# A new order, planned buffers and TensorE transposes of x in a fused attention and gated FFN kernel

## The chip, the cores and the metric

The kernel runs on one NeuronCore of a Trainium2 chip. The metric is device time in microseconds (us). Three runs of the kernel before took 385.79, 387.66 and 388.32 us; the median is 387.66 us. A separate profiled execution gives the trace that is read below. The core has TensorE (PE: matrix products into eight PSUM banks), VectorE (DVE), ScalarE (ACT), GpSimd (POOL) and SyncE (SP), which here only issues DMAs. Each engine works through its own instruction list strictly in the order that the program gives; semaphores make it wait for others.

## What is computed

A linear attention with an exponential feature map, then a gated FFN (ReLU gate times value). Shapes: q, k, v are 8 batches x 8 heads x 576 positions x 64; the feature width is 128 (256 with the mirrored half); the FFN goes 512 to 1536 to 512 on 4608 rows.

```python
def phi(x):
    proj = np.einsum('bhsd,df->bhsf', x, w_phi)
    proj = proj - np.max(np.abs(proj), axis=-1, keepdims=True)
    return np.concatenate([np.exp(proj), np.exp(-proj)], axis=-1)
q_p, k_p = (phi(q), phi(k))
kv = np.einsum('bhsf,bhsd->bhfd', k_p, v)
z = np.sum(k_p, axis=2)
num = np.einsum('bhsf,bhfd->bhsd', q_p, kv)
den = np.einsum('bhsf,bhf->bhs', q_p, z)[..., None] + 1e-06
x = (num / den).transpose(0, 2, 1, 3).reshape(B * S, H * D)
out = (np.maximum(x @ w_gate, 0.0) * (x @ w_val)) @ w_out
```

## The kernel before

The whole program is one long word list, `ORDER`. Each word names a step, its indices and the PSUM banks that it uses; `kr.1.0:0672` is step `do_kr` for batch 1, head group 0, in banks 0, 6, 7 and 2. The last lines of the kernel walk the list and call the steps, and that order is the order of every engine's instruction list and of every DMA queue. Nothing else schedules. Buffers are rings: the n-th use of a tile name takes tile n modulo the ring's size.

A batch has 512 main positions (four tiles of 128) and 64 left over; the leftovers of two batches make one mixed tile, called batch 8. So the FFN has nine groups of 512 rows: batches 0 to 7 and group 8. Heads come in groups of 2, 3 and 3.

The steps of one batch, with the engine that does each:

- Loads. POOL issues those of k (`lk`), q (`lq`), their leftovers (`lm`, `ln`), v of batch 0 (`lv.0`), and the weights in thirds: `wl.0.i` is third i of `wv`, `wl.1.i` of `wg` (512 of 1536 columns each), `wo.i` third i of `wo`. SP issues v of the other batches (`lv`), its leftovers (`lw`), and `gt`, a small transfer that the next k load on POOL waits for. v of batch 1 lands in a free part of the tile that later holds x transposed (`xTs`).
- k features. DVE transposes k in blocks (`kt`, `ku`), PE multiplies by w_phi (`kr`), ACT takes exponentials with both signs (`ke`), DVE takes the maximum of absolute values (`kx`), ACT turns it into scales (`kk`), POOL scales v with them (`vs`, `vr`, and `vo` for the column of ones). For batch 0 PE transposes k itself (`k0`), DVE copies it from PSUM (`k1`), PE multiplies (`k2`), and DVE scales one head group (`kp` on ACT, `vd` and `vp` on DVE).
- kv (`kv`, PE), copied from PSUM by ACT (`kc`) or DVE (`kd`).
- q features. `qt` (DVE transpose), `qc` or `qs` (PE), `qe` (ACT), `qx` (DVE maximum), then `qy` (PE), `qz`, `qu` (DVE) and `qw` (ACT), which give the factor between the two halves. `mt` to `mw` are the same for the mixed tile.
- Numerator and denominator, per position tile i and head group: `nu` (PE), `nt` and `nv` (DVE combine the two halves), `nr` (DVE reciprocal), `nx` (normalise on POOL) or `ny` (the same on DVE) writes tile `xu`.
- x transposed to `xTs`: `xt` is a DMA transpose issued by SP. For batch 0, tiles 0 and 1, it is PE (`xp`, four 128x128 transposes into a PSUM bank) and a copy by DVE (`xc`).
- FFN. `fv` and `fg` are the products with a column block f (128 wide) of `wv` and `wg`, four matmuls of 512 columns each; f 8 to 11 lie in the last third of the weights. `va` copies the value product from PSUM (ACT), `ga` multiplies it with the rectified gate (DVE) into a slot of `h2` (15 slots, taken in turn). For batch 0, blocks 0 to 7 are done per position tile (`pv`, `pg`, `pa`, `pb`: 16 matmuls of 128 columns each), so that they can start before all of x is there; blocks 8 to 11 go as `fv` and `fg` and need all four tiles of x. `fo.g.t.part` is a third of the output product of tile t, `oc` copies it from PSUM (ACT), `od` writes it out (SP). A tile of group 8 is written in two DMAs of 64 rows.
- `zz.n` issues n matmuls on a tile of zeros, with no use made of the result.

The order around the change at the start, PE's list alone: `xp.0.0`, `pg.0.0`, `xp.0.1`, ..., `pv.1.2`, `pg.1.2`, `fv.0.9`, `fv.0.8`, `pv.0.3`, `qc.1.0`, ... The tiles 2 and 3 of x of batch 0 are turned by `xt.0.2` and `xt.0.3`; on SP's list three loads of batch 1's v stand between those two. At the end, group 7 comes before group 8: the last words are `fo.8.2.2`, `oc.8.2`, `od.8.2`.

Of the kernel before, what the change touches and what calls it, by code (L numbers as in the profile page):

```python
# [9 lines left out]
BF16 = mybir.dt.bfloat16  # L10
# [18 lines left out]
qy.0.0:5 qz.0.0:5 qe.0.0.1.1:6 kv.0.2:3 qx.0.0.3:2 kv.0.1:5 qe.0.1.3.0:7 qu.0.0 qe.0.0.1.0:6
qe.0.1.1.1:0 qx.0.1.2:1 kc.0.2:3 qw.0.0 kc.0.1:5 qx.0.1.3:7 wl.0.1 vs.0.0.1 qy.0.1:6 qz.0.1:6  # L30
kt.1.1 nu.0.0.2:0 vs.0.0.0 nt.0.0.2:0 qe.0.1.2.1:1 vo.0 kv.0.0:3 qe.0.1.2.0:1 kc.0.0:3
qe.0.0.3.0:2 qu.0.1 nv.0.0.2:0 qy.0.2:6 qz.0.2:6 qw.0.1 nu.0.0.1:5 nt.0.0.1:5 qe.0.1.3.1:7
qe.0.0.2.1:4 nu.0.1.1:1 nu.0.0.0:0 qu.0.2 qw.0.2 nv.0.0.1:5 qy.0.3:3 qz.0.3:3 nu.0.1.0:6 zz.2:2
kr.1.1:2537 nt.0.0.0:0 lm.1.0 nt.0.1.0:6 qe.0.0.2.0:4 nv.0.0.0:0 nt.0.1.1:1 ke.1.1.2.0:3 lq.1.2
wl.1.1 nu.0.1.2:0 nr.0.0 nu.0.2.2:4 nv.0.1.1:1 ny.0.0 nt.0.1.2:0 ke.1.1.1.0:5 nv.0.1.0:6
ke.1.1.3.0:7 ke.1.1.0.0:2 ke.1.1.1.1:5 lw.1.0 nv.0.1.2:0 zz.2:1 xp.0.0:1 wl.0.2 xc.0.0:1
nt.0.2.2:4 nr.0.1 nx.0.1 ke.1.1.2.1:3 nu.0.2.0:6 nu.0.2.1:0 qu.0.3 qw.0.3 nt.0.2.0:6 ke.1.1.3.1:7
nv.0.2.2:4 nv.0.2.0:6 ke.1.1.0.1:2 nt.0.2.1:0 pg.0.0:1 kx.1.1.1:5 nv.0.2.1:0 kx.1.1.2:3 pv.0.0:4
xp.0.1:6 nr.0.2 nx.0.2 xc.0.1:6 xt.0.2 pv.1.0:5 nu.0.3.0:0 pa.0.0:4 pb.0.0:1 pa.1.0:5 ln.0.1
pv.0.1:3 pa.0.1:3 lv.1.0 qt.1.1 kx.1.1.3:7 pg.0.1:4 nt.0.3.0:0 kx.1.1.0:2 kk.1.1.0 nv.0.3.0:0  # L40
pb.0.1:4 nu.0.3.1:6 qc.1.1:1537 qe.1.1.0.0:1 nu.0.3.2:2 qe.1.1.0.1:1 nt.0.3.1:6 qe.1.1.1.0:5
nt.0.3.2:2 qe.1.1.3.0:7 nv.0.3.1:6 pv.1.1:0 lv.1.3 nv.0.3.2:2 pg.1.1:4 pa.1.1:0 lv.1.1 nr.0.3
qx.1.1.0:1 qe.1.1.2.0:3 ln.0.0 qe.1.1.1.1:5 qx.1.1.3:7 qe.1.1.3.1:7 pg.1.0:6 pv.0.2:2 nx.0.3 ku.1
pa.0.2:2 xt.0.3 qe.1.1.2.1:3 pg.0.2:1 pb.1.0:6 kt.1.0 kr.1.0:0672 ke.1.0.1.0:6 wo.2 qx.1.1.1:5
wl.1.2 ke.1.0.3.1:2 pb.1.1:4 qx.1.1.2:3 ke.1.0.0.0:0 ke.1.0.2.1:7 ms.1 ke.1.0.2.0:7 kx.1.0.1:6
ke.1.0.1.1:6 pv.1.2:5 lm.2.0 lm.2.1 pb.0.2:1 pa.1.2:5 vs.1.1.0 wo.0 ke.1.0.0.1:0 pg.1.2:4
kx.1.0.3:2 ke.1.0.3.0:2 qt.1.0 fv.0.9:3 kk.1.1.1 kx.1.0.0:0 fv.0.8:1 pv.0.3:6 va.0.9:3 pb.1.2:4
qc.1.0:5203 vs.1.1.1 va.0.8:1 pa.0.3:6 kt.1.2 qx.1.0.1:2 kx.1.0.2:7 qe.1.0.3.0:3 qx.1.0.3:3 lk.2.3
wo.1 pv.1.3:4 qe.1.0.0.0:5 qx.1.0.0:5 qe.1.0.1.0:2 kk.1.0.0 vr.1.1.0 vs.1.0.0 vr.1.0.0
qe.1.0.1.1:2 kk.1.0.1 vo.1.0 vs.1.0.1 qe.1.0.3.1:3 pg.0.3:1 pb.0.3:1 vr.1.1.1 qe.1.0.0.1:5  # L50
pg.1.3:6 vr.1.0.1 qx.1.0.2:0 pa.1.3:4 mt.0 lv.2.3 pb.1.3:6 qe.1.0.2.0:0 fv.0.10:7 kr.1.2:2315
kx.1.2.1:3 fg.0.10:4 ke.1.2.3.1:5 kx.1.2.0:2 fv.0.11:6 qe.1.0.2.1:0 qy.1.0:0 va.0.10:7 kx.1.2.2:1
# [36 lines left out]
va.1.7:2 ga.1.7:0 vr.3.0.1 nx.2.1 fg.1.9:6 ga.1.9:6 nr.2.0 kx.3.1.1:3 ke.3.1.2.0:4 nu.2.3.2:2
ke.3.1.3.1:7 ke.3.1.0.1:1 vr.3.1.1 nx.2.0 ln.2.0 kx.3.1.3:7 ln.2.1 nu.2.3.0:4 fv.1.11:5 kt.4.0  # L90
# [146 lines left out]
def kernel(  # L237
# [11 lines left out]
    nc = tc.nc  # L249
# [730 lines left out]
```

## Time and profile before

| | before |
|---|---|
| median of three runs | 387.66 us |
| profiled execution, span from first to last instruction | 384.0 us |
| instructions | 9108 |
| PE busy (weight loads apart) | 365.5 us, 95%, 3551 matmuls |
| DVE busy | 275.2 us, 72%, 651 |
| ACT busy | 237.0 us, 62%, 566 |
| POOL busy | 160.1 us, 42%, 179 |
| moved by DMA | 38.29 MB |
| mean granted TensorE clock | 0.974 |

The three runs differ by 0.7%, and the profiled execution's span is 3.7 us below their median. Busy times are sums over the whole span and hide that its parts differ, so the table of busy time by stretch is of more use. In it and in the time line, each row begins with microseconds from the first instruction; in the time line the second number is the length, the bracket at the end of a row tells how long the engine stood idle before it and whose work ended that. A merged row (x8) holds that many instructions. A matmul's row is longer than the time it keeps the array, since its end overlaps the next; the distance from start to start tells the rate.

### The profile page before, as it was taken

The numbers are of one execution on the slowest core, as the hardware profiler recorded it, in microseconds if no ns is written. First come the engines' busy times: TensorE is split into PE (matmuls) and PEld (weight loads), VectorE is DVE, ScalarE is ACT, GpSimd is POOL, SyncE is SP. The second block draws the span as 40 slices with busy tenths as digits, with TensorE's granted clock in tenths as the row PEclk, the third lists the DMA queues.
The fourth block names the chain that finished last, engine by engine and source line by source line (L and its number), as shares of the span: only waits on it lengthen the run. The fifth ranks groups of instructions, "written<-read, shape, count | busy, mean of one in ns | idle before, by whom it ended". The sixth has DMA issues, their size and how long they took to land.

```text
span 384.0 us, 9108 instructions
## 1 busy us (share of the span) xinstructions
PE 365.5 (95%) x3551; PEld 193.7 (50%) x3551; DVE 275.2 (72%) x651; ACT 237.0 (62%) x566; POOL 160.1 (42%) x179
## 2 busy tenths in 40 slices
PE   7699679999999999999999999999999999999994
PEld 4268646545544554455545544464445544444442
DVE  4979929999997898788957797798667822521320
ACT  2987849788867915985787647964977213321321
POOL 8593729587366423672393025811462120100000
PEclk9869979999999999999999999999999999999998
DMA  8999999995965765677335742552410031000114
GB/s 131 231 167 183 181 179 154 131 127 81 215 54 124 114 106 81 122 116 109 77 88 93 134 83 65 111 102 56 112 55 2 3 82 56 27 15 0 55 63 103
DMA packets 91456, 38.29 MB, mean 100 GB/s; under 512 B 65302, under 2 KB 86550, under 8 KB 91414
## 3 DMA queue, kind: packets, MB, share of 16 engines
q0 software_dynamic: 33904, 15.23, 30.6%
q1 hardware_dynamic: 57510, 22.49, 27.4%
q8 instruction: 28, 0.46, 0.5%
q14 instruction: 14, 0.11, 0.1%
HBM read 37.95 MB, written 9.44 MB: 123 GB/s over the span
## 4 chain that ended last, share of the span: by engine, by line
PE 85%; DVE 6%; DMA 4%; SPq 1%; issue 1%; POOL 1%; ACT 0%; DVEq 0%; POOLq 0%
PE bank L865 45%; PE bank L920 25%; PE bank L618 6%; PE bank L717 3%; DMA xTs<-xu 2%; PE bank L654 2%; PE bank L476 2%; DMA qn<-in_q_dram 2%; DVE mk L531 1%; DVE t L738 1%; DVE u L748 1%; PE bank L891 1%; SPq L424 1%; DVE maxq L677 1%; PE bank L852 1%
## 5 line engine op out<-in xcount | busy, mean ns | idle before, releaser
L880 ACT CAST val<-bank 128x512 bf16<-128x512 f32 x100 | 58.0, 599 | 77.3 <-PE bank L865 56.4
L883 DVE SCALAR_TENSOR_TENSOR h<-bank,val 128x512 bf16<-128x512 f32 x100 | 66.7, 678 | 50.3 <-PE bank L865 37.0
L920 PE MATMUL bank<-wo,h 128*128 128x512 bf16 x432 | 99.0, 379 | 0.0
L523 ACT ACTIVATE kp<-bank 128x384 bf16<-128x384 f32 x192 | 81.9, 517 | 20.1 <-PE bank L476 8.3
L865 PE MATMUL bank<-xTs,wv 128*128 128x512 bf16 x352 | 88.2, 384 | 5.9 <-DMA xTs<-xu 5.7
L760 POOL TENSOR_TENSOR xu<-u,r 128x512 bf16<-128x512 f32 x35 | 36.4, 1043 | 124.4 <-DVE r L756 81.7
L865 PE MATMUL bank<-xTs,wg 128*128 128x512 bf16 x352 | 87.9, 379 | 0.0
L669 ACT ACTIVATE qp<-bank 128x512 bf16<-128x512 f32 x128 | 70.7, 627 | 4.4 <-PE bank L654 3.7
L920 PEld LDWEIGHTS <-h 128*128 128x128 bf16 x432 | 40.8, 98 | 47.7 <-issue 0.9
L865 PEld LDWEIGHTS <-wv 128*128 128x128 bf16 x400 | 37.1, 98 | 47.9 <-issue 9.7
L578 POOL TENSOR_TENSOR vs<-vn,ek 128x780 bf16<-128x780 f32 (+3 forms) x40 | 53.0, 1341 | 18.7 <-ACT ek L540 12.2
L865 PEld LDWEIGHTS <-wg 128*128 128x128 bf16 x400 | 36.6, 98 | 42.0 <-issue 3.3
L677 DVE TRANSPOSE_TENSOR_REDUCE maxq<-bank 128x16 f32<-128x512 f32 x64 | 42.4, 692 | 16.8 <-ACT val L906 7.3
L531 DVE TENSOR_REDUCE mk<-bank 128x3 f32<-128x384 f32 x96 | 49.3, 542 | 7.0 <-ACT kp L523 4.6
L929 ACT COPY ob<-bank 128x512 f32<-128x512 f32 x36 | 21.4, 598 | 29.9 <-PE bank L920 26.6
L748 DVE TENSOR_TENSOR u<-bank,t 128x195 f32<-128x195 f32 (+1 forms) x108 | 34.3, 332 | 2.7
L738 DVE TENSOR_TENSOR t<-bank,cq 128x195 f32<-128x195 f32 (+1 forms) x96 | 30.1, 327 | 3.2 <-PE bank L717 2.1
L717 PEld LDWEIGHTS <-qp 128*128 128x128 bf16 x512 | 23.8, 99 | 11.6 <-issue 0.6
L717 PE MATMUL bank<-kv,qp 128*128 128x65 bf16 x512 | 26.4, 195 | 0.2
L597 POOL TENSOR_TENSOR vr<-vm,ek 64x260 bf16<-64x260 f32 x32 | 19.7, 618 | 16.7 <-issue 9.8
L618 PEld LDWEIGHTS <-kp 128*128 128x128 bf16 x640 | 24.1, 102 | 3.3 <-DVE h L883 0.2
L618 PE MATMUL bank<-vs,kp 128*128 128x65 bf16 x512 | 24.3, 199 | 0.0
(81 smaller groups left out, 317.9 us busy)
## 6 DMA issues: line engine op xcount, KB each, us to landing
out_dram<-ob SPq DMA_DIRECT2D x32, 256.0 KB, 2.2
vn<-in_v_dram SPq DMA_DIRECT2D x24, 256.0 KB, 4.6
kn<-in_k_dram POOLq DMA_DIRECT2D x7, 512.0 KB, 8.4
qn<-in_q_dram POOLq DMA_DIRECT2D x7, 512.0 KB, 6.2
wg<-in_moe_w_gate_dram POOLq DMA_DIRECT2D x3, 512.0 KB, 8.4
wv<-in_moe_w_val_dram POOLq DMA_DIRECT2D x3, 512.0 KB, 8.6
wo<-in_moe_w_out_dram POOLq DMA_DIRECT2D x3, 512.0 KB, 13.3
vm<-in_v_dram SPq DMA_DIRECT2D x16, 64.0 KB, 4.1
```

The source lines that it names most:

```text
L523: nc.scalar.activation(kp_of(3 * b + j)[:, i, s].rearrange("p n f -> p (n f)"), bank[bk[0]][:, 0 : 3 * F], AF.Exp, scale=(1.0, -1.0)[s],)
L531: nc.vector.tensor_reduce(mk_of(3 * b + j)[:, :, i], bank[bk[0]][:, 0 : 3 * F].rearrange("p (n f) -> p n f", f=F), axis=AX.X, op=ALU.max, ...
L578: nc.gpsimd.tensor_tensor(vs_of(3 * b + j)[:, s, 0:n].rearrange("p n i e -> p (n i) e")[:, :, 0:e], src[:, lo:hi].rearrange("p h i e -> p ...
L618: nc.tensor.matmul(out_ps[:, h - lo, s, :], lhsT=lhsT, rhs=rhs, start=(at == 0), stop=(at == 2 * n * (C + 1) - 1),)
L669: nc.scalar.activation(qp_of(4 * b + i)[:, s, 4 * hq : 4 * hq + 4].rearrange("p h m -> p (h m)"), bank[bk[0]], AF.Exp, scale=(1.0, -1.0)[s],)
L677: nc.vector.tensor_reduce(maxq[:, :, i, 4 * hq : 4 * hq + 4].rearrange("p t h -> p h t"), bank[bk[0]].rearrange("p (h t u) -> p h t u", h= ...
L717: nc.tensor.matmul(bank[bk[0]][:, E * n : E * (n + 1)], lhsT=qp_of(4 * b + i)[:, s, h, :], rhs=kv_of(b)[:, h, s, :],)
L748: nc.vector.tensor_tensor(u_of(serial(b, i))[:, lo:hi], parts(bk, n)[:, :, 0], t_of(3 * serial(b, i) + g)[:, 0:n], op=ALU.add,)
L865: nc.tensor.matmul(bank[bk[0]], lhsT=w[:, dc, P * f : P * f + P], rhs=xT(g)[:, dc, :], start=(dc == 0), stop=(dc == NDC - 1),)
L880: nc.scalar.copy(val_of(NFC * g + f), bank[bk[0]])
L883: nc.vector.scalar_tensor_tensor(h2_of(g, f), bank[bk[0]], 0.0, val_of(NFC * g + f), op0=ALU.max, op1=ALU.mult)
L920: nc.tensor.matmul(bank[bk[0]], lhsT=h2_of(g, f)[:, P * t : P * t + P], rhs=wo_sb[:, f, :], start=(f == 0), stop=(f == NFC - 1),)
```

## The change

All 2040 words are put in a new order and get other banks; 2044 words come out. What differs in the steps themselves:

- Words carry buffers: `ke.0.1.1.0:1@kp0` tells which tile of a ring this use takes. The rings keep their sizes, the choice of a tile is written out. The slots of `h2` are chosen the same way (`@hs3`), apart from batch 0's twelve.
- x of batch 0: `xp.0.2`, `xp.0.3` replace `xt.0.2`, `xt.0.3`, and all four tiles are copied from PSUM by ACT (`xa`, new) instead of DVE (`xc`). `nx.0.0` replaces `ny.0.0`.
- Work moved between engines: 25 of the 100 `va` go to DVE (`vb`, new), 13 of the 36 `oc` (`oe`, now used); 12 of 18 `kd` on DVE become `kc` on ACT; six `nx` become `ny` (DVE).
- The fill `zz` has 69 matmuls instead of 42: 37 instead of 22 at the very start, 10 and 5 around the last k group of batch 0 instead of 4 and 0.
- Group 8's products are put among those of groups 6 and 7, and `fo.7.2` is the last output tile. It is copied in two halves of 256 columns, one by ACT (`o1`), one by DVE (`o2`), and written by two DMAs, one issued by SP (`d1`), one by ACT (`d2`).
- The loads move: on POOL `wl.0.2` from before `nx.0.1` to behind `nx.0.2`, `lm.1.0` and `vo.1.1`; `wl.1.2`, `wo.0` follow `nx.0.3`; `wo.1`, `wo.2` come behind `lk.2.3`. On SP `lv.1.0`, `lv.1.3` come right behind `lv.1.2`.

PE's list at the start after the change: `xp.0.0`, `kr.1.1`, ..., `pg.0.0`, `pv.1.0`, `xp.0.1`, ..., `xp.0.2`, ..., `xp.0.3`, `pv.1.2`, `kr.1.0`, `pg.1.2`, `pv.0.3`, `fv.0.9`, `fv.0.10`, ...

```diff
+    fresh = {}
+
     def ring(name, n, shape, dtype):
         tiles = [sb.tile(shape, dtype, name=f"{name}_{i}", tag=f"{name}_{i}") for i in range(n)]
-        return lambda i: tiles[i % n]
+        at = {}
+
+        def of(i):
+            if n == 1:
+                return tiles[0]
+            if i not in at:
+                at[i] = fresh.pop(name)
+            return tiles[at[i]]
+
+        return of
...
+    def do_xa(bk, b, i):
+        nc.scalar.copy(
+            xT_cols(b, i),
+            bank[bk[0]].bitcast(BF16)[:, 0 : NDC * P].rearrange("p (a b) -> p a b", b=P),
+        )
...
     def h2_of(g, f):
-        return h2[:, (NFC * g + f) % NH2]
+        i = NFC * g + f
+        if i not in h2_at:
+            h2_at[i] = fresh.pop("hs")
+        return h2[:, h2_at[i]]
...
+    def do_vb(bk, g, f):
+        nc.vector.tensor_copy(val_of(NFC * g + f), bank[bk[0]])
...
+    def do_o1(bk, g, t):
+        nc.scalar.copy(ob_of(4 * g + t)[:, 0:HD], bank[bk[0]][:, 0:HD])
+
+    def do_o2(bk, g, t):
+        nc.vector.tensor_copy(ob_of(4 * g + t)[:, HD:DM], bank[bk[0]][:, HD:DM])
+
+    def do_d1(bk, g, t):
+        r0 = S * g + P * t
+        nc.sync.dma_start(out=out[r0 : r0 + P, 0:HD], in_=ob_of(4 * g + t)[:, 0:HD])
+
+    def do_d2(bk, g, t):
+        r0 = S * g + P * t
+        nc.scalar.dma_start(out=out[r0 : r0 + P, HD:DM], in_=ob_of(4 * g + t)[:, HD:DM])
...
     for word in ORDER.split():
+        word, _, slots = word.partition("@")
         name, _, banks = word.partition(":")
         name, *args = name.split(".")
+        fresh.clear()
+        for slot in filter(None, slots.split(",")):
+            fresh[slot.rstrip("0123456789")] = int(slot[len(slot.rstrip("0123456789")) :])
```

More of the change, by code (lines that the diff above doesn't have):

```diff
@@ L227 @@
[L227 to L232 removed]
+ms.0 wp ms.6 lk.0.1 wc lq.0.1 wq ms.4@vr0 ms.3@vr1 id ms.2 wd zz.37:0 k0.1:0 k1.1:0@kT0 zz.5:1
@@ new lines @@
+qs.0.1.0:5 qt.0.0@qT1 kx.0.2.3:7 vs.0.1.1@vs0 ke.0.2.3.1:7 ke.0.0.0.0:0 ke.0.0.3.0:6 kx.0.0.3:6@mk0
+ke.0.0.1.0:3 kp.0.2.1:7 kp.0.2.0:7 kx.0.0.1:3 kx.0.0.0:0 lk.1.3 ke.0.0.0.1:0 wl.0.1 ke.0.0.1.1:3
+kx.0.0.2:2 kk.0.0.1@ek1 qs.0.0.2:1 qx.0.0.2:1 vs.0.1.0 qs.0.0.1:0 vp.2:7@vs1 kk.0.0.0
+qe.0.1.3.1:4@qp1 vd.0.2.1:7 qx.0.0.1:0 ke.0.2.3.0:7 qs.0.0.0:3 qe.0.0.0.1:3@qp2 qx.0.1.0:5
+qe.0.1.0.0:5 ke.0.0.3.1:6 wl.0.0 ke.0.0.2.1:2 qx.0.0.0:3 qe.0.1.0.1:5 vd.0.2.0:7 qs.0.0.3:6
+qe.0.0.0.0:3 qe.0.0.2.1:1@qp3 qe.0.0.1.1:0 lv.1.2 qy.0.0:2 qe.0.0.3.0:6 qx.0.0.3:6 qs.0.1.2:5
@@ new lines @@
+kx.1.1.1:3 pa.0.0:0@val1 kk.1.1.1@ek1 kk.1.1.0 xa.0.2:7 qt.1.1@qT0 ms.1 pv.0.1:1 pb.0.0:2
+pa.0.1:1@val2 pb.0.1:5 nu.0.3.1:0 nt.0.3.1:0@t0 qc.1.1:7346 qe.1.1.3.1:6@qp3 nu.0.3.2:1
+nt.0.3.2:1@t1 qe.1.1.2.1:4@qp1 pv.0.2:2 pa.0.2:2@val2 qe.1.1.0.0:7@qp0 nv.0.3.2:1 qe.1.1.0.1:7
+pg.1.0:5 kt.1.0@kT0 qe.1.1.3.0:6 nv.0.3.1:0 vo.1.1@vs2 nr.0.3@r0 qe.1.1.1.0:3@qp2 qx.1.1.3:6
+pv.1.1:2 wl.0.2 lv.1.1 nx.0.3@xu0 pg.1.1:0 pa.1.1:2@val1 xp.0.3:6 qx.1.1.0:7 lw.1.0 xa.0.3:6
+qe.1.1.1.1:3 ln.0.1 pb.1.0:5 ku.1 pv.1.2:7 pa.1.2:7@val0 lm.2.0 kr.1.0:6251 ke.1.0.1.1:2@kp0
@@ new lines @@
+xt.8.1 ln.2.0 qx.4.1.0:1 qx.4.1.1:2 vb.3.0:0@val1 fv.3.1:7 vb.3.1:7@val0 qe.4.1.3.1:5 vr.4.1.0
+vr.4.0.1 kv.4.0:1 vs.4.2.1@vs0 vs.4.1.1 fv.3.4:0 xt.8.0 od.2.1 fv.3.10:7 ga.3.0:3@hs5 fv.3.5:3
+kk.4.2.0 qx.4.1.3:5 va.3.4:0@val1 qx.4.1.2:4 qy.4.0:4 qz.4.0:4@my1 kv.4.1:0 ga.3.1:6@hs8
+kd.4.1:0@kv0 qu.4.0@mz0 ln.2.1 qe.4.1.1.0:2 vs.4.2.0 kv.4.2:4 kc.4.0:1 nu.4.0.0:0 va.3.5:3@val3
+kd.4.2:4 qw.4.0@cq0 nt.4.0.0:0@t2 qe.4.1.1.1:2 fg.3.4:6 nu.4.1.1:4 nu.4.1.2:2 nv.4.0.0:0@u0
+ga.3.4:6@hs10 fv.3.11:0 nt.4.1.2:2@t2 nv.4.1.2:2@u1 nt.4.1.1:4@t1 va.3.10:7@val0 nu.4.0.1:6
@@ new lines @@
+ke.5.1.1.0:5 fg.3.8:2 ga.3.10:3@hs7 fo.3.0.0:4 ke.5.1.1.1:5 nx.4.2@xu3 kx.5.1.0:0 kk.5.1.0@ek2
+vr.5.0.1@vr0 kr.5.2:0357 ke.5.2.0.0:0@kp2 ke.5.2.0.1:0 ke.5.2.1.1:3 qt.5.1@qT0 fo.3.1.1:1
+kx.5.2.3:7@mk2 ke.5.2.2.1:5 xt.4.1 ke.5.2.2.0:5 xt.4.2 ke.5.2.1.0:3 ga.3.8:2@hs11 fo.3.0.1:4
+fo.3.2.1:6 qt.5.0@qT1 fo.3.2.2:6 kx.5.2.2:5 fo.3.0.2:4 kx.5.2.0:0 kx.5.2.1:3 kk.5.2.1@ek1
+oe.3.2:6@ob1 kt.6.0 fo.3.1.2:1 oe.3.1:1@ob0 ke.5.2.3.0:7 od.3.1 qc.5.0:6305 vs.5.0.1@vs0
+ke.5.2.3.1:7 qe.5.0.1.1:3@qp0 kk.5.1.1 oc.3.0:4@ob2 fv.4.6:7 kt.6.1@kT1 vb.4.6:7@val2 qx.5.0.2:0
@@ L233 @@
+fo.7.2.2:1 o1.7.2:1@ob2 d1.7.2 o2.7.2:1 d2.7.2
 """
@@ L501, in do_k1, with do_kw @@
         nc.vector.tensor_copy(
+            kT_of(j).rearrange("p n m a -> p (n m a)"), bank[bk[0]].bitcast(BF16)[:, 0 : 6 * P]
+        )
+    def do_kw(bk, j):
+        nc.scalar.copy(
             kT_of(j).rearrange("p n m a -> p (n m a)"), bank[bk[0]].bitcast(BF16)[:, 0 : 6 * P]
@@ L793, in do_xc @@
         )
+    def do_xa(bk, b, i):
+        nc.scalar.copy(
+            xT_cols(b, i),
+            bank[bk[0]].bitcast(BF16)[:, 0 : NDC * P].rearrange("p (a b) -> p a b", b=P),
+        )
     def do_mt(bk, p):
@@ L856, in do_mn @@
                     )
+    h2_at = {f: f for f in range(NFC)}
     def h2_of(g, f):
-        return h2[:, (NFC * g + f) % NH2]
+        i = NFC * g + f
+        if i not in h2_at:
+            h2_at[i] = fresh.pop("hs")
+        return h2[:, h2_at[i]]
     def ffn_in(bk, g, f, w):
@@ L906, in do_pa, with do_pc @@
         nc.scalar.copy(val_of(4 * pk + qd), bank[bk[0]])
+    def do_pc(bk, pk, qd):
+        nc.vector.tensor_copy(val_of(4 * pk + qd), bank[bk[0]])
     def do_pb(bk, pk, qd):
```

431 lines of the change are left out of this document (215 added, 216 removed).

## Prediction

> **What bounds the kernel now.** I read the table of busy time by stretch first, then the waits of TensorE, then the time line and the chain of waits around the longest wait, then the tail. Busy time by stretch (columns: us, PE, PE weight loads, DVE, ACT, POOL, granted PE clock, DMA share, GB/s):
>
> ```profile
> 0.00:10.00 10.00, 7.42 (x56) 4.98 (x57) 4.92 (x12) 2.92 (x5) 8.39 (x17) 1.00 0.89 138
> 10.00:20.00 10.00, 5.65 (x51) 2.32 (x51) 10.00 (x20) 9.62 (x29) 5.81 (x7) 0.80 1.22 226
> 30.00:40.00 10.00, 9.61 (x168) 8.52 (x166) 9.96 (x32) 7.24 (x19) 3.96 (x5) 1.00 1.32 180
> 40.00:50.00 10.00, 4.65 (x98) 4.27 (x95) 8.03 (x16) 6.33 (x16) 8.90 (x10) 0.84 1.19 176
> 60.00:80.00 20.00, 20.00 (x288) 11.73 (x287) 19.61 (x58) 16.37 (x47) 14.12 (x18) 1.00 1.09 136
> 100.00:140.00 40.00, 39.81 (x410) 20.83 (x409) 35.05 (x86) 27.77 (x68) 19.92 (x21) 1.00 0.78 124
> 220.00:260.00 40.00, 40.00 (x426) 20.73 (x424) 34.61 (x83) 27.18 (x64) 17.49 (x17) 1.00 0.43 87
> ```
>
> From 60 us on TensorE is busy without a gap, at full clock. There a new order can only lose. What can be won lies before 60 us (10.00 to 20.00 is DVE's and ACT's; 40.00 to 50.00 has TensorE half idle) and in the tail. The waits of TensorE (us in total, times, longest) name one large item:
>
> ```profile
> PE bank L865 <- DMA xTs<-xu: 5.7, 1, 5.7
> PE bank L654 <- DVE qT L645: 2.2, 1, 2.2
> ```
>
> The time line around it:
>
> ```profile
> 39.52 1.04 POOL L760 TENSOR_TENSOR xu<-u,r 128x512 bf16<-128x512 f32 x1 [2.58 <-DVE r L756]
> 43.59 1.06 PE L891 MATMUL bank<-xTs,wg 128*128 128x128 bf16 x16
> 50.31 3.50 PE L865 MATMUL bank<-xTs,wv 128*128 128x512 bf16 x8 [5.66 <-DMA xTs<-xu]
> 55.37 0.72 DVE L677 TRANSPOSE_TENSOR_REDUCE maxq<-bank 128x16 f32<-128x512 f32 x1 [7.34 <-ACT val L906]
> ```
>
> and the chain of waits:
>
> ```profile
> 40.71 9.46 DMA xTs<-xu
> 50.31 3.50 PE bank L865 x8
> ...
> 58.05 0.86 PE bank L865 x4
> ```
>
> The last x tile of batch 0 is ready at 40.56; its DMA transpose is issued at 40.71 among the loads of v and weights and lands 9.46 us later. TensorE has nothing else in its order, and DVE, waiting in its own order for the product behind, stands 7.34 us. Then eight matmuls of fv take 3.50 us, 438 ns each, where four at 58.05 take 216 ns each.
>
> The tail:
>
> ```profile
> 372.86 8.01 SPq L941 DMA_DIRECT2D out_dram<-ob  x8
> 379.15 0.59 ACT L929 COPY ob<-bank 128x512 f32<-128x512 f32 x1 [1.14 <-PE bank L920]
> ```
>
> After the last matmul come one copy of 0.59 and two output DMAs issued one behind the other on SP (eight such took 8.01 with waits; the single rows show 0.578 median).
>
> **The change, part by part.** Times below are against the profiled execution, span 384.0.
>
> *First matmuls.* The idle fill zz grows from 42 to 69 matmuls, 37 of them (not 22) ahead of the first transposes of k. The 22 took 4.88, 213 ns apart; the next matmuls, at 6.63, were at full clock. Fifteen more last 1.6 (at 109 ns) to 3.2 us (at 213), so the fill ends at 7.5 to 9.1 and the first k, landed at 6.59, waits about 1 to 2.5 us; nearer to 1, since the clock was up by 6.63. DVE's first long work, qT, starts at 8.45 after q's landing and stays about there, so the kx work slips 0.3 us and ACT's first ke (8.28) about 1 us. Counting each queued DVE operation at the mean of its row, DVE has 24.75 us up to nr.0.0 (the first tile's reciprocal) instead of 26.6. On POOL vs.0.0.0 (1.04) and a copy of 0.28 now stand ahead of the four vr (2.59 in all, from 20.08): kv.0.2 starts near 24 instead of 22.1, but its last part no longer waits for vs.0.0.0. I put the first transposes of x (xp.0.0), at 30.74 before, at 31.4: bounds 30.0 (kv at full clock, 30 matmuls in 0.95 as at 94.22, instead of 1.65) and 32.5.
>
> *Batch 0 on TensorE.* Two DMA transposes go; xp.0.2 and xp.0.3 come, 8 matmuls of 56 ns, 0.45 us. Their copies xa are on ACT, for which no row exists: below, DVE's 0.396 (L790), above, ACT's 0.599 (L880); I take 0.6, and four make 2.4 us of ACT. From xp.0.0 TensorE was nearly dense: 13.1 us of matmuls, at full-clock spacing, in the 13.9 us to 44.65. Now the stretch from xp.0.0 to fv.0.9 holds 14.1 (plus xp, plus pv.0.3 brought forward), so 14.9 with the same 0.8 of small gaps: fv.0.9 starts at 46.3 instead of 50.31, **-4.0**. DVE allows that: nr.0.3, done at 39.44, has 38.1 us of rows ahead of it instead of 38.8. ACT hardly does: up to xa.0.3 it has 39.9 us of rows, and before it got through 37.3 by 39.50; at that pace, started 1 us later, xa.0.3 ends at 43 and pv.1.2, kr.1.0, pg.1.2 and pv.0.3 (3.2) follow in part: 45 to 47.
>
> *Clock.* The eight matmuls behind the wait cost 8 x 0.216 = 1.73 at full clock instead of 3.50. I count that as won, since no wait is left in the forecast: **-1.8**. If a wait of a few us stays there, the trace does not show which clock follows a shorter wait than 5.66; the bounds are 0 and -1.8. The Trainium skill ("TensorE: Matmul & The Clock Gate", "What's actually happening") says that an idle window of about 3.4 us sends TensorE back to half clock; the wait of 5.66 agrees, and by that rule any wait under about 3.4 keeps the whole 1.8. The same section counts the warm-up in time, not in matmuls, so by it the fifteen extra fill matmuls buy nothing; the row at 6.63, at full clock after 22, agrees, and the sum has them as a cost already.
>
> *Loads.* SP loses two transposes, so v of batch 1 (issued 36.96 to 39.06) goes out largely before 25. The POOL queue moves the last third of wv (wl.0.2) from 27.97 to behind nx.0.2, a load of k's rest and vo.1.1, which waits for ACT's kk.1.1.0 (before at 37.37): issue near 38. Behind vo.1.1 on POOL stands nx.0.3 too, but its own input (nr.0.3, 39.4) is later than that. The three wv loads landed after 8.6 in the median; the rows run from 6.1 to 10.0, and the wg load issued at 41.32 took 11.5. So it lands at 44 to 49.5, and fv.0.9 needs it at 46.3. With v out of the way I take 7 to 8, 45.5: no wait. wo's last third is issued near 53 and lands by 66 even at 13.3, before fo.0.1.2 at about 67. lk.2.3 goes out at about the same time (48.3 before), its 14.3 us to landing shortened by the megabyte of v ahead of it gone; kt.2.0 wants it near 59. On SP a load of batch 2's v waits for a memset in DVE's order (near 35); only loads and transposes of later batches are behind it.
>
> *Middle.* 25 val copies (vb), 13 output copies (oe) and net 5 normalisations (ny) go to DVE, 12 kv copies and 2 xc leave it. A DVE copy of a full bank has no row: between 0.499 (kv, 390 columns) and 0.678 (L883); I take 0.6. 25 x 0.6 + 13 x 0.6 + 5 x 0.68 - 12 x 0.499 - 2 x 0.396 = 19.4 us more for DVE. But up to kr.3.0 DVE has 4 us less than before by the rows, and from there to kr.7.2 some 12 more: 134 busy of the 160 us from 100 to 260 become about 145. Covered by TensorE's dense work as long as no bank waits for DVE. ACT and POOL lose 14 and 5 us. Planned buffers add no instruction; they only move waits for a free buffer. The mixed tiles' products (fv.8) now come before those of batch 7: its last x needs nt, nv, nr, ny (1.6), a DMA issue of 1.2 and 2.5 to landing, and TensorE has eleven groups of 0.864 between, 9.5 us: hidden. For waits that the new order brings after fv.0.9 (0 to 4; before it 0.2 to 0.35 each, few) I take **+1.2**.
>
> *Tail.* The last tile is plain, in halves on ACT and DVE. No row has 256 columns of a copy; ACT's 128x256 exp is 0.41, its copy of 512 columns 0.59, so 0.4 is taken and 0.2 is saved; the two DMAs go out on two queues, saving one issue of 0.5: **-0.7**. If the DMA from ACT costs more, this is nothing.
>
> Sum: -4.0 - 1.8 + 1.2 - 0.7 = -5.3, span 378.7. The median of runs stands 3.7 above the profiled span (387.66 and 384.0): **382.4 us**, 1.4% faster.
>
> **Rivals.**
>
> *The weights take the wait's place.* wl.0.2 takes 11.5 us like the wg load, fv.0.9 starts at 49.5, having waited 3.2, and the eight matmuls stay slow. For: it is issued 10 us later, into the busiest DMA stretch. Against: two transposes and most of v are gone from there. Gain 0.8 + 0.7: span 382.5, time 386.2; with no gain in the tail either, 386.9.
>
> *DVE becomes what TensorE waits for* (the slower side). Each of the 25 vb holds a bank until DVE, strictly in order, reaches it; DVE is at 19.61 of 20 from 60 to 80 already. If each makes TensorE wait for one such copy, 25 x 0.6 = 15 us: 384.0 - 6.5 + 15 = 392.5, time 396. It is slower by 1% from 10.4 us, 0.42 each. Against: TensorE waited for DVE 0.2 us (u) in all after 60, and DVE's added work lies mostly after 100 where it had 26 us free.
>
> *Cleaner than forecast.* xp.0.0 at 30.0 and no new waits: -5.4 - 1.8 - 0.7 = -7.9, time 379.8.
>
> **How the numbers follow.** About 1% (3.9 us) can be told from no change. Forecast 0.55, of which 0.09 falls within 1% (a new wait of 3 us does that); cleaner 0.15; weights 0.18; DVE 0.12. Faster 0.46 + 0.15 = 0.61, same 0.09 + 0.18 = 0.27, slower 0.12. The range takes in the cleaner case with 1 us below it and the weights case with 2 us above: 378.5 to 388.5, leaving out DVE's case and some.
>
> **What would show it.** Right: no wait of TensorE on xTs before 60, fv.0.9 (the first L865 matmuls; new line number) at 45 to 47.5 and 216 ns each, DVE's 7.34 gone, 20.00 of 20 for TensorE from 60 on, 4.2 instead of 4.9 us from the last matmul to the end. Wrong: a wait on wv at that place, TensorE waiting for val or ob copies by DVE between 100 and 260, or a first transpose of x after 33.

## The result: 6.9% slower, and the profile after

The changed kernel took 413.41 us (median of four runs, 413.26 to 413.53), the kernel before 386.73 in the runs beside them: a ratio of 1.0691, 95% interval 1.0636 to 1.0746. The profiled execution's span is 411.5 us instead of 384.0. From the page of the changed kernel, the busy times and the chain of waits by engine:

```profile
PE 377.0 (92%) x3534; PEld 200.3 (49%) x3586; DVE 305.2 (74%) x681; ACT 228.8 (56%) x544; POOL 155.5 (38%) x174
...
PE 58%; DVE 22%; ACT 14%; issue 5%; DVEq 0%; ACTq 0%
```

The chain of the kernel before:

```profile
PE 85%; DVE 6%; DMA 4%; SPq 1%; issue 1%; POOL 1%; ACT 0%; DVEq 0%; POOLq 0%
```

There 85% of the chain was TensorE's own work and 6% DVE's. Now 36% is work of DVE and ACT. Yet neither is full. Busy time by stretch, with the columns of the table in the prediction:

```profile
30.00:40.00 10.00, 9.12 (x169) 8.17 (x167) 8.45 (x30) 7.26 (x19) 3.48 (x4) 0.78 1.18 174
40.00:50.00 10.00, 9.32 (x160) 8.31 (x157) 8.86 (x22) 8.80 (x21) 4.48 (x6) 1.00 0.46 61
60.00:80.00 20.00, 18.40 (x265) 11.24 (x266) 17.30 (x48) 14.73 (x39) 12.44 (x16) 1.00 1.04 135
220.00:260.00 40.00, 35.37 (x382) 18.57 (x388) 29.16 (x74) 22.34 (x53) 11.58 (x12) 1.00 0.51 88
```

From 220 to 260 all three engines are less busy than before (TensorE 35.37 instead of 40.00, DVE 29.16 instead of 34.61, ACT 22.34 instead of 27.18). When all three idle more, the question is for whom each of them waits.

What was aimed at did come. TensorE's rows where the last tile of x of batch 0 is turned (L822) and where fv.0.9 starts (L916):

```profile
49.13 0.38 PE L822 MATMUL bank<-ident,xu 128*128 128x128 bf16 x4 [0.23 <-DVE maxq L717]
...
53.22 1.89 PE L916 MATMUL bank<-xTs,wv 128*128 128x512 bf16 x7
```

The wait on xTs is gone, and fv.0.9 runs at full clock. But it starts at 53.2 instead of 50.3, since the first transpose of x starts at 36.7 instead of 30.7.

A table over the whole span sorts this out. At the start of a named step: the time, less what TensorE's products before it take at full clock (four matmuls of 512 columns 0.864 us, and so on; fill counts as lost). What is left is time in which TensorE did not get on.

| us lost by | xp.0.0 | fv.0.9 | mc.0 | kr.3.0 | kr.5.0 | kr.7.0 | last matmul |
|---|---|---|---|---|---|---|---|
| before | 20.9 | 27.3 | 29.2 | 29.7 | 30.9 | 31.7 | 31.8 |
| after | 27.5 | 29.8 | 33.1 | 36.7 | 45.8 | 56.6 | 60.1 |

6.6 us are lost up to the first transpose, 2.7 won back by mc.0 (near 65 us), and 24.4 more are lost from there to the end, where the kernel before lost 2.6. With 0.5 of added transposes and 1.3 less in the tail this makes the 27.5 us. No single wait of TensorE there is longer than 1.7 us. The trace shows 14.8 us of them (52 of 3586 matmul records are missing from it): 9.5 end behind DVE, 4.8 behind ACT, 0.5 behind neither. In the kernel before they are 0.2 us.

The waits of DVE and ACT tell what sort they are. Four rows of the changed kernel (us in total, times, longest), where ke writes kp and qe writes qp on ACT, kx writes mk and qx writes maxq on DVE:

```profile
DVE mk L571 <- ACT kp L563: 16.5, 20, 1.8
...
ACT kp L563 <- DVE mk L571: 9.5, 12, 1.8
...
DVE maxq L717 <- ACT qp L709: 8.8, 9, 2.4
...
ACT qp L709 <- DVE maxq L717: 5.5, 10, 1.2
```

The same four of the kernel before:

```profile
DVE mk L531 <- ACT kp L523: 4.6, 5, 1.6
DVE maxq L677 <- ACT qp L669: 3.4, 5, 1.7
ACT kp L523 <- DVE mk L531: 2.9, 7, 0.9
...
ACT qp L669 <- DVE maxq L677: 0.4, 1, 0.4
```

40.3 us instead of 11.3. These are sums of waits of two engines, not time lost by the kernel. kx needs nothing that ke makes, and ke nothing of kx: both only read the product in the bank. They wait because the program lets two engines read one bank only one after the other, in the order of its words. I call this a hand-off. One place, the product kr.5.1 in banks 0, 5, 2 and 6, in the time line of the changed kernel:

```profile
203.20 1.26 ACT L563 ACTIVATE kp<-bank 128x384 bf16<-128x384 f32 x3 [0.28 <-PE bank L511]
205.74 1.64 ACT L563 ACTIVATE kp<-bank 128x384 bf16<-128x384 f32 x4 [1.29 <-DVE mk L571]
...
204.48 0.56 DVE L571 TENSOR_REDUCE mk<-bank 128x3 f32<-128x384 f32 x1 [0.96 <-ACT kp L563]
204.96 0.30 DVE L500 STREAM_TRANSPOSE kT<-km 128x128 f32<-128x128 f32 x1
205.18 0.52 DVE L571 TENSOR_REDUCE mk<-bank 128x3 f32<-128x384 f32 x1
...
206.28 1.02 PE L977 MATMUL bank<-wo,h 128*128 128x512 bf16 x4 [1.09 <-ACT kp L563]
```

ACT's list is ke on banks 0, 6, 2, then 6 again. DVE's list is kx on bank 2, a transpose for the next batch, kx on bank 6. DVE stands 0.96 us until ACT's third ke leaves bank 2. ACT then stands 1.29 us until DVE has left bank 6, behind kx on bank 2 and the transpose. TensorE stands 1.09 us for bank 6, which ACT's fourth ke reads last. Each engine had work for other banks behind the waiting word.

The tail, ACT's and DVE's halves of the last tile:

```profile
407.97 0.37 ACT L1005 COPY ob<-bank 128x256 f32<-128x256 f32 x1 [2.00 <-PE bank L977]
...
408.38 0.42 DVE L1008 COPY ob<-bank 128x256 f32<-128x256 f32 x1 [3.21 <-ACT ob L1005]
```

Here too: one bank, so the halves come one after the other.

### The profile page after: what moved, and what is told of

It is laid out like the page before. It is cut to its first block, busy times and chain, and to the rows that moved or that the text cites. A ratio compares the mean times of both kernels' runs of the same rounds, so it can differ in the third digit from the quotient of the medians.

```text
span 411.5 us, 9129 instructions
## 1 busy us (share of the span) xinstructions
PE 377.0 (92%) x3534; PEld 200.3 (49%) x3586; DVE 305.2 (74%) x681; ACT 228.8 (56%) x544; POOL 155.5 (38%) x174
## 4 chain that ended last, share of the span: by engine, by line
PE 58%; DVE 22%; ACT 14%; issue 5%; DVEq 0%; ACTq 0%
PE bank L916 29%; PE bank L977 15%; ACT qp L709 6%; ACT kp L563 5%; PE bank L658 5%; DVE mk L571 4%; DVE t L778 3%; DVE maxq L717 3%; DVE u L788 3%; DVE h L937 3%; PE bank L757 2%; PE bank L694 2%; PE bank L511 2%; PE bank L408 2%; DVE xu L800 1%
## 5 line engine op out<-in xcount | busy, mean ns | idle before, releaser
L916 PE MATMUL bank<-xTs,wg 128*128 128x512 bf16 x340 | 86.9, 379 | 5.2 <-ACT qp L709 1.3
L931 ACT CAST val<-bank 128x512 bf16<-128x512 f32 x75 | 43.8, 591 | 82.2 <-PE bank L916 66.4
L916 PE MATMUL bank<-xTs,wv 128*128 128x512 bf16 x333 | 84.6, 379 | 3.1 <-DVE h L937 0.8
L800 POOL TENSOR_TENSOR xu<-u,r 128x512 bf16<-128x512 f32 x30 | 31.1, 1040 | 130.0 <-DVE r L796 107.7
L571 DVE TENSOR_REDUCE mk<-bank 128x3 f32<-128x384 f32 x96 | 50.1, 546 | 16.7 <-ACT kp L563 16.5
L916 PEld LDWEIGHTS <-wg 128*128 128x128 bf16 x400 | 37.2, 98 | 48.4 <-issue 9.0
L916 PEld LDWEIGHTS <-wv 128*128 128x128 bf16 x400 | 37.6, 98 | 46.4 <-issue 5.9
L618 POOL TENSOR_TENSOR vs<-vn,ek 128x780 bf16<-128x780 f32 (+3 forms) x40 | 52.8, 1337 | 15.8 <-ACT ek L580 15.2
L637 POOL TENSOR_TENSOR vr<-vm,ek 64x260 bf16<-64x260 f32 x32 | 19.8, 625 | 18.7 <-ACT ek L580 15.3
L986 ACT COPY ob<-bank 128x512 f32<-128x512 f32 x22 | 13.0, 593 | 22.9 <-PE bank L977 21.3
```

The lines of the kernel that those rows point to most:

```text
L571: nc.vector.tensor_reduce(mk_of(3 * b + j)[:, :, i], bank[bk[0]][:, 0 : 3 * F].rearrange("p (n f) -> p n f", f=F), axis=AX.X, op=ALU.max, ...
L618: nc.gpsimd.tensor_tensor(vs_of(3 * b + j)[:, s, 0:n].rearrange("p n i e -> p (n i) e")[:, :, 0:e], src[:, lo:hi].rearrange("p h i e -> p ...
L916: nc.tensor.matmul(bank[bk[0]], lhsT=w[:, dc, P * f : P * f + P], rhs=xT(g)[:, dc, :], start=(dc == 0), stop=(dc == NDC - 1),)
L931: nc.scalar.copy(val_of(NFC * g + f), bank[bk[0]])
```

## The experiments

Three theories. A: the hand-offs, that is the order in which ACT and DVE take the banks. B: DVE's added work, the slower rival of the prediction. C: the planned banks and buffers leave no slack. The expectations use a replay: every engine's list run in order, each operation with the start-to-start distance of its row in the two traces, between engines the least delay seen there, waits for banks, buffers and hand-offs as the words demand, no clock gate, and loads at usual times. It is an estimate, and its figures are no measurements; it gives 412 for the changed kernel (411.5 in the trace) and 372 for the one before (384.0, of which 5.7 is the xTs wait and 1.8 the slow clock that it does not know; 4.5 stay unexplained).

| run | us, median | ratio to before, 95% interval |
|---|---|---|
| changed kernel | 413.41 | 1.0636 to 1.0746 |
| its maxima out of SBUF | 386.04 | 0.9987 to 1.0044 |
| the same in the kernel before | 387.29 | 0.9999 to 1.0067 |
| its engine moves undone | 425.54 | 1.0962 to 1.1086 |
| the moves alone, in the old order | 396.23 | 1.0216 to 1.0322 |
| its ACT and DVE lists re-sorted | 398.08 | 1.0248 to 1.0420 |
| re-sorted again | 395.76 | 1.0228 to 1.0347 |
| that, ny.8.1 on POOL | 391.52 | 1.0070 to 1.0348 |
| its k maxima out of SBUF | 396.91 | 1.0236 to 1.0330 |
| its q maxima out of SBUF | 410.16 | 1.0593 to 1.0740 |
| kernel before, x by TensorE | 379.81 | 0.9810 to 0.9877 |
| that, last tile on two queues | 379.60 | 0.9819 to 0.9905 |
| that sorted up to mc.0, last tile in halves | 381.94 | 0.9863 to 0.9924 |

**The hand-offs taken away.** In the changed kernel, and as a control in the kernel before, DVE's maxima read constants of the same shape:

```diff
 def do_kx(bk, b, j, i):
-    bank[bk[0]][:, 0 : 3 * F].rearrange("p (n f) -> p n f", f=F),
+    identf[:, None, :].to_broadcast([P, 3, F]),
 def do_qx(bk, b, hq, i):
-    bank[bk[0]].rearrange("p (h t u) -> p h t u", h=4, u=R),
+    still.rearrange("p (h t u) -> p h t u", h=4, u=R),
```

(do_mx likewise; `still` is one SBUF tile that holds w32f, w64f and identf.)

> The changed kernel, but the maxima on DVE (kx, qx, mx) read constants in SBUF of the same shape instead of the PSUM bank; their count, order and size stay, the maxima of the projections are left out. No bank is then read by both ACT and DVE in those steps. Theory A (hand-offs on the banks): 385 to 393 us, since the replay falls by 26 us to 386. Theory B (DVE's load): DVE's list is as long as before, so 408 us or more. Theory C (banks held too long): banks come free a little earlier, some us: 405 to 412.

> The control to the run with the maxima elsewhere: the same edit (kx, qx, mx read constants in SBUF; the maxima are left out) in the kernel before. Theory A: the order of the kernel before hardly waits at the hand-offs, the replay gains 0.4 us, so 383 to 388 us, within 1% of the kernel before. If reading PSUM by DVE is dear in itself (theory D: the maxima are slower out of PSUM, whatever the order), this one gains as much as the changed kernel did.

386.04 and 387.29 us. The changed kernel gains 27.4 us by this edit, the kernel before nothing, though DVE's list has the same 681 operations in the same order (297.9 us busy instead of 305.2). From the page of the changed kernel with the edit:

```profile
PE 371.7 (96%) x3586; PEld 197.5 (51%) x3586; DVE 297.9 (77%) x681; ACT 224.9 (58%) x544; POOL 155.5 (40%) x174
...
PE 75%; DVE 10%; ACT 4%; DMA 4%; issue 3%; POOL 2%; DVEq 0%; POOLq 0%; ACTq 0%
```

and its stretch from 220 to 260, where TensorE has its 40 us back at the same load of DVE:

```profile
220.00:260.00 40.00, 39.92 (x418) 20.61 (x417) 34.26 (x83) 26.10 (x63) 16.99 (x17) 1.00 0.39 69
```

This edit does more than take the hand-offs away. Each bank comes free a little earlier, DVE's maxima no longer wait for TensorE's product, and one long DVE operation, ny.8.1, shrinks from 3.61 to 0.78 us (more on it below; the stretch from kr.4.0 to kr.5.0, in which it lies, gives 3.5 of the 27.4 us). So alone it doesn't show that the order of the reads is what costs; the re-sorted lists below change only the order. The Trainium skill ("PSUM — Partial Sum Buffer", "PSUM bank collisions raise a hardware error") says that two engines must not touch the same bank and quadrant at one time, two readers included, and that software has to keep them apart. The rows at 203 to 206 show reads kept apart in this way; no run here let two engines read one bank at once.

**The engine moves.** Undone in the new order, and done alone in the old one:

```diff
-kc.2.0:4@kv0
-oe.1.0:2@ob1
-vb.2.0:3@val0
+kd.2.0:4@kv0
+oc.1.0:2@ob1
+va.2.0:3@val0
...
```

> The changed kernel in its own order, but every moved operation back on the engine of the kernel before: 25 val copies and 13 output copies on ACT, 12 kv copies on DVE, the normalisations as before. Nothing is left out. Theory B (the work added to DVE is what costs): DVE gets back about 19 us of work, so 388 to 398 us. Theory A (hand-offs in the order of ACT and DVE): no gain, since the order stays; with ACT's lists longer rather a loss, 411 to 424 us. Theory C: within 3 us of 413.

> The kernel before in its own order, with the moves of the change between engines alone: 25 val copies and 13 output copies to DVE, 12 kv copies to ACT, six normalisations to DVE. Nothing is left out. Theory A (order and engine choice belong together; moved work in an order that was not made for it meets waits): slower, 392 to 400 us, the replay gives 13 us more. If the moves cost nothing in themselves: 384 to 388 us. Theory B (DVE's load is what costs in the changed kernel): it should cost here nearly as much as there, 405 us or more.

425.54 and 396.23 us. Theory B falls as the cause of the 27 us: with DVE's busy time down from 305.2 to 281.7 us (and ACT's up from 228.8 to 243.6) the kernel is 12 us slower, and the four rows of hand-off waits grow to 46.8 us. In the old order the same moves cost 10 us, though DVE is as busy there (297.1) as in the fast run with the constants (297.9). Engines and order belong together: the new order is slower without the moves than with them, and the moves are slower in the old order than none. But those 10 us are not hand-offs of these four kinds, whose rows come to 13.0 us there instead of 11.3. TensorE's waits for val copies by DVE, the slower rival's own mechanism, are 2.5 us of them; the rest stays open.

**The lists re-sorted.** Only ACT's and DVE's lists change, with TensorE's list, banks and buffers kept. The readers of kr.5.1 in ACT's and DVE's lists, in the second version:

```diff
-ACT ke.5.1.0.0:0 ke.5.1.3.0:6 ke.5.1.2.1:2 ke.5.1.3.1:6 ke.5.1.0.1:0 ke.5.1.2.0:2
-DVE kx.5.1.2:2 ku.6 kx.5.1.3:6 ga.3.9:7 kx.5.1.1:5
+ACT ke.5.1.3.0:6 ke.5.1.2.0:2 ke.5.1.3.1:6 ke.5.1.0.1:0 ke.5.1.2.1:2 ke.5.1.1.0:5
+DVE kx.5.1.2:2 kx.5.1.3:6 ku.6 ga.3.9:7 kx.5.1.1:5
```

> The changed kernel with only the order inside ACT's list and inside DVE's list changed (most of their words moved by some places). TensorE's, POOL's and SP's lists, all banks, all buffers and which engine does what stay as in the changed kernel. Nothing is left out. Theory A (hand-offs: the reads of one PSUM bank by ACT and by DVE go strictly one after the other in the order of the program, and the new order makes the two engines wait for each other all the time, which TensorE then pays): 381 to 392 us, since a replay of the lists, made of the spacings and delays of the rows of the two traces, gives a span of 380 for it where it gives 412 for the changed kernel (411.5 in the trace). Theory B (DVE has too much work): the work is the same, so 405 us or more. Theory C (banks and buffers are planned too tightly): they are the same, so 405 us or more.

> The re-sorting of ACT's and DVE's lists once more, TensorE's, POOL's and SP's lists, banks, buffers and engines as in the changed kernel; this time only from the first normalisation of batch 0 on, with the start left as in the changed kernel, and with a replay that knows how long an operation of DVE waits for the one just before it. Nothing is left out. Theory A (the order in which ACT and DVE take the banks is what costs, and the first attempt fell short by DVE's w64f wait at the start and by a replay too coarse): 385 to 393 us. Rival (a re-sorted list can give back no more than the first attempt did; the rest is in TensorE's order and the banks): 396 to 402 us.

398.08 and 395.76 us: both miss theory A's range, and the second lies 0.24 under its rival's. The hand-off waits fall from 40.3 to 14.0 us in the second, and 17.6 of the 27.4 us come back with nothing changed but the order inside ACT's and DVE's lists (of all their words, not of the readers of kr alone). So the order of the two lists is worth that much, and theory C can have at most the rest. The sum of the hand-off waits is no measure of the time, though: it is 9.6 us in the first version, less than in the second, and the first is no faster. The first begins with a 6.4 us wait of DVE for w64f, but TensorE is not late by it: it starts fv.0.9 at 52.8 us there and at 53.0 in the second. In the second, TensorE takes 37.2 us from kr.4.0 to kr.5.0, no less than in the changed kernel (36.6). DVE's rows in one place there, POOL's, and TensorE's:

```profile
171.75 3.65 DVE L803 TENSOR_TENSOR xu<-u,r 128x512 bf16<-128x512 f32 x1
175.32 0.68 DVE L937 CAST val<-bank 128x512 bf16<-128x512 f32 x1
```

```profile
169.72 2.94 POOL L621 TENSOR_TENSOR vs<-vn,ek 128x780 bf16<-128x780 f32 x2
172.60 0.72 POOL L445 DMA_DIRECT2D qm<-in_q_dram  x1
173.33 1.50 POOL L621 TENSOR_TENSOR vs<-vn,ek 128x780 bf16<-128x780 f32 x1
174.77 0.75 POOL L439 DMA_DIRECT2D km<-in_k_dram  x1
```

```profile
176.05 2.32 PE L919 MATMUL bank<-xTs,wv 128*128 128x512 bf16 x7 [2.96 <-DVE val L937]
```

The first DVE row is ny.8.1, one of the six normalisations that the change moved to DVE; an undisturbed one took 0.69 us. TensorE stands 2.96 us for the val copy behind it, and then has a granted clock of 0.50 from 178 to 180 us. One more edit:

```diff
-ny.8.1@xu2
+nx.8.1@xu2
```

> The second re-sorting once more, with a single further edit: the normalisation of the mixed tile 1 (ny.8.1) on POOL again (nx.8.1) instead of on DVE. Nothing is left out. In the trace of the second re-sorting this one DVE operation took 3.65 us instead of 0.69, from 171.75 to 175.40, while POOL ran four operations without a gap beside it. If DVE is held up there by POOL's use of SBUF and TensorE pays for it (it fell 5.3 us behind between kr.4.0 and kr.5.0, where the replay loses 0.8): 391 to 393.5 us, against 395.76. Rival (TensorE would have waited there anyway): 395 to 397 us.

391.52 us, 4.2 less, as expected. The intervals of the two ratios overlap, but the runs don't (390.29 to 392.50 against 394.82 to 396.96), and in the traces the stretch from kr.4.0 to kr.5.0 takes 32.7 us instead of 37.2: the long operation was on TensorE's path. In the changed kernel itself ny.8.1 took 3.61 us, and TensorE waited 1.74 us behind it; what it cost there was not tried alone.

**k and q apart.** The first edit for kx alone and for qx alone (mx reads the bank in both):

> The changed kernel, but only the maxima of the k features (kx) read a constant in SBUF instead of the bank; those maxima are left out, the q ones (qx) still read the bank. Theory A: the hand-offs of both kinds add up, and the replay puts 15 of the 25 us on those of k: 396 to 401 us. Rival (the two kinds wait for the same things, and either alone would do): 386 to 391 us, or 410 and more if those of q alone decide.

> The counterpart to the run with the k maxima elsewhere: in the changed kernel only the maxima of the q features (qx) read a constant in SBUF; those maxima are left out, kx still reads the bank. Theory A (the two kinds add up; 16 of 27 us went with those of k): 401 to 406 us. Rival (they overlap, each alone gives most of it): 395 to 399 us.

396.91 and 410.16 us, 16.5 and 3.3 us less than the changed kernel. The first is as expected, the second a miss of both ranges: the two gains come to 19.8, not 27.4. It is not that the waits of k grew when those of q went: the two rows of k are 16.3 and 9.8 us, instead of 16.5 and 9.5. The trace with the q maxima in SBUF is 4.3 us ahead of the changed kernel at kr.4.0 (149.6 against 153.9 us) and no longer at kr.5.0 (190.7 against 190.5). Between them stand ny.8.1 on DVE and a wait of TensorE:

```profile
173.33 5.87 DVE L801 TENSOR_TENSOR xu<-u,r 128x512 bf16<-128x512 f32 x1
```

```profile
181.04 1.44 PE L917 MATMUL bank<-xTs,wv 128*128 128x512 bf16 x3 [5.07 <-DVE val L935]
```

ny.8.1 was held up for longer than in the changed kernel (3.61 us), TensorE waited 5.07 us instead of 1.74, and the granted clock was 0.50 behind it, up to 184 us. So the small gain says little of the hand-offs of q; without that place it would be nearer to 8 us (3.3 and about 4.5, an estimate from these starts).

**The good part alone.** In the words of the kernel before:

```diff
-xt.0.2 ... xt.0.3
+xp.0.2:1 pa.0.1:3 xa.0.2:1 ... xp.0.3:0 xa.0.3:0
```

> The kernel before, with one part of the change alone: x tiles 2 and 3 of batch 0 turned by TensorE (xp) and copied by ACT (xa) instead of by DMA. All other words, banks and buffers as before; nothing is left out. Theory A (the part is good, the new order spoils it): TensorE's wait of 5.66 us on xTs and the slow matmuls behind it (1.8) go, 1.1 us of new work in the lists comes: 379 to 383 us, 1 to 2% faster than before. Rival (another wait, such as the weights wl.0.2 or a copy by ACT, takes its place): 385 to 388 us, no change.

379.81 us, 1.6% faster than the kernel before. Its time line around the place of the old wait:

```profile
43.61 0.52 PE L482 MATMUL bank<-w,kT 32*128 32x128 bf16 x24 [0.67 <-ACT xTs L807]
...
45.86 1.89 PE L887 MATMUL bank<-xTs,wv 128*128 128x512 bf16 x8
```

fv.0.9 starts at 45.9, and the eight matmuls take 1.89 instead of 3.50. Lost by the last matmul: 25.3 us, 6.5 less than before. Two additions to this:

> The kernel before with x of batch 0 turned by TensorE (as in the run with that part alone, nothing else sorted), and the two DMAs of the last output tile issued by two engines, SP and ACT, instead of one behind the other on SP; the tile is still copied whole by ACT. Nothing is left out. Theory A: one DMA issue of 0.6 us less at the end: 378.5 to 380.5 us, 1.5 to 2% faster than the kernel before. If the DMA issued by ACT costs as much as it saves: as the run with x alone, 379.5 to 381.5.

> The run before with x turned by TensorE, and in addition: its words of TensorE, ACT, DVE and POOL up to mc.0 sorted with the replay, with the reads of one bank by ACT and DVE kept in turn, and the last output tile copied in two halves (ACT and DVE) and written by two DMAs from SP and ACT. Nothing is left out. Theory A with the replay right within 3 us: 2 to 4 us under the run with x alone, 376 to 381 us. If the replay is too coarse at the start, where loads set the pace: within 1 us of that run.

The first differs from the run above by

```diff
-for bb in range(2): nc.sync.dma_start(...)
+for bb, eng in ((0, nc.sync), (1, nc.scalar)): eng.dma_start(...)
```

the second also by the order of the words up to mc.0 and by `o1`, `o2` for `oc` of the last tile. 379.60 us for the first: no difference that can be told from the run with x alone, but both are faster than both kernels. The second took 381.94 us, 2 us more where 2 to 4 less were expected. Sorted so, TensorE waits 3.30 us at 17 us where the run with x alone waits 2.24. From 20 to 30 us, first the sorted run:

```profile
20.00:30.00 10.00, 8.30 (x103) 5.95 (x102) 6.66 (x13) 6.48 (x15) 7.65 (x11) 0.50 1.21 194
```

then the one with x alone:

```profile
20.00:30.00 10.00, 9.49 (x150) 7.05 (x150) 8.03 (x26) 8.44 (x22) 8.97 (x13) 0.68 1.18 192
```

Half clock throughout instead of 0.68, and 103 matmuls instead of 150: the replay knows no clock. That this is what cost the 2 us is read from these rows and was not tried.

## Why the prediction was wrong

**The step that failed** is "For waits that the new order brings after fv.0.9 (0 to 4; before it 0.2 to 0.35 each, few) I take +1.2". By the table TensorE lost 25.8 us more than before behind the start of fv.0.9 (28.3 less 2.5), 24.4 of them from mc.0 on. The term rested on the sentence "Covered by TensorE's dense work as long as no bank waits for DVE", and that on sums of DVE's and ACT's rows over long stretches. A sum by engine does not see that a bank with two readers ties their lists together word by word. The profile of before had the sign in it: 11.3 us of waits between ke and kx, qe and qx, and taking them away there changed nothing (387.29 us). They were covered by that order, and the order was what the change replaced. With the order inside ACT's and DVE's lists alone changed, 17.6 us came back. The premise "There a new order can only lose" was right; the price was not.

**The slower rival** had the sign and another mechanism. TensorE's waits for val copies by DVE are 0.4 us in the trace, and taking all the moves back made it worse. That its 396 us meet another kernel, the moves in the old order (396.23), is mostly luck: the rival has 15 us of waits for val copies, and that trace has 2.5.

**First transpose of x at 31.4 (30.0 to 32.5)**: 36.7, one of the signs of being wrong that the prediction names. The fill cost what was said (first k at 8.0 instead of 6.6), but kv.0.2 started at 28.6, not near 24. With the maxima out of SBUF xp.0.0 starts at 33.6, so 3.1 of the 5.3 us go with that edit. DVE's 4.00 us wait for w32f (its third word now) stands in the same stretch; what it and the fill cost was not tried alone.

**fv.0.9 at 46.3, -4.0**: 53.2 in the changed kernel, 1.6 us beyond what the late xp.0.0 explains. With the transposes alone in the old order it was 45.9: this term was sized rightly for what it described.

**Clock, -1.8**: right. No wait of us is left there, and the eight matmuls run at full clock. But the sentence that the trace does not show the clock behind a shorter wait than 5.66 overlooks a row of its own list: behind the 2.2 us wait for qT, at 16.7 us, the granted clock falls to 0.52 (16 to 18 us) and is 0.50 up to 26. TensorE had been little used before it (0.47 of the 2 us from 14 on). And in the run re-sorted again a wait of 2.96 us in a dense part was followed by half clock. That any wait under about 3.4 us keeps the whole 1.8 is not borne out by these rows.

**Loads**: wl.0.2 was issued at 44.03, not near 38, and landed at 49.43, ahead of fv.0.9 at 53.2. The rival of the weights falls, but with luck: that landing would have been too late for fv.0.9 at 46.3, as forecast. Both were late, so TensorE did not wait.

**Tail, -0.7**: 3.60 us from the last matmul to the end instead of 4.86, so -1.3, though the two halves took 0.83 one behind the other where one whole copy takes 0.59. The gain is behind the copies (2.68 us to the end instead of 4.23). Halves and two queues are not what brings it: in the sorted run of the old order, which has both, the stretch from the last matmul is 4.54 us, and 4.50 with x alone. What remains of the change there is the plain tile at the end, which was not tried alone. So the sign was right, and the source that was named for it is not what the runs show.

**What stays open.** With the maxima out of SBUF the changed kernel still loses 8.8 us from mc.0 on, against 2.6. The replay without any wait for banks is 8 us shorter than without hand-offs only. That would fit banks reused too soon (theory C), but it is the replay's estimate, and no run tried it. Order and ny.8.1 together gave back 21.9 of the 27.4 us (391.52); how the rest divides between hand-offs that are left, banks that come free earlier and maxima that no longer wait for TensorE is not shown.

## What to carry to other kernels

Where two engines read the same PSUM bank, treat their lists as one: after any reordering, follow for each bank who reads it when, and look for waits in both directions between engines that need nothing of each other. Before pricing a new order by busy sums, look for waits that the old order merely covers; here they were what came to the surface. A large change is best taken apart: here the one edit that removed the long wait gains 1.6% alone, and the changed kernel is 8.6% slower than that (the ratios 1.0691 and 0.9844).

## What the runs showed of the hardware

- A DVE operation with both inputs in SBUF (ny, fp32 128x512, else 0.69 us) was held up while POOL worked: 3.65 us in the row above, ending 0.57 after POOL's vs of 173.33; 3.61 in the changed kernel; 5.87 in the run with the q maxima in SBUF. The Trainium skill ("SBUF — State Buffer", "SBUF: two separate sides") says that DVE with two SBUF inputs and a GpSimd operation that reads SBUF share a port pair that one of them locks for a whole instruction. The trace agrees that DVE is shut out, but it can be for longer: in the runs with 3.65 and 5.87 us the 0.67 us that POOL spent on issuing a DMA between two vs did not let it through. In the changed kernel it ended in such a gap, at 181.32; why there is not shown.
- Two copies of 256 columns out of one bank by two engines (0.37 and 0.42 us) came one after the other, DVE's waiting for ACT's; one of 512 columns takes 0.59.
- Behind waits of TensorE of 2.96 and 5.07 us in otherwise dense stretches the granted clock was 0.50 for a while (178 to 180 us, and 180 to 184 us, in the two runs); behind one of 1.74 us (changed kernel, at 182.00) it stayed at 1.00.
- At the start the clock can stay low for long: 0.50 from 18 to 30 us in the run sorted up to mc.0, from 18 to 26 in the run with x alone. The waits before differ (3.30 and 2.24 us at 17 us, and 1.58 us at 22 in the sorted run alone); which of them decides is not shown.
